# Top-k attention with a ReLU MLP: values as the stationary operand, mask and norm steps on GpSimd, half batches at both ends

## The chip, the cores and the metric

One NeuronCore of a Trainium2 chip runs the whole kernel in one launch. The metric is the time of one execution on the device in microseconds (us). The engines are called by their names in the profile: PE is TensorE (matrix products), DVE is VectorE, ACT is ScalarE, POOL is GpSimd, SP is SyncE, which here only issues DMAs.

## The reference

The attention has 8 batches, 8 heads, 576 tokens and a head size of 64, all float32. Each query keeps the 32 largest of its 576 scores.

```python
scores = scale * np.matmul(q, k.transpose(0, 1, 3, 2))           # 8 x 8 x 576 x 576
kth = np.partition(scores, -32, axis=-1)[..., -32:-31]
scores = np.where(scores >= kth, scores, -1e9)
attn = np.exp(scores - np.max(scores, axis=-1, keepdims=True))
attn = attn / (np.sum(attn, axis=-1, keepdims=True) + 1e-09)
x = heads_side_by_side(np.matmul(attn, v))                       # 8 x 576 x 512
xn = (x - mean(x)) / np.sqrt(var(x) + 1e-06) * g_ln              # over the 512
out = x + np.maximum(xn @ w_ch1, 0.0) @ w_ch2                    # 512 -> 2048 -> 512
```

The two weights come as float64 and are turned to float32 on the chip, word by word.

## The kernel before

**Units.** Two heads of one batch make a pair; there are 32 pairs. A pair has five units: four full query tiles of 128 rows (two score tiles each, one a head) and a rest unit, in which the last 64 rows of both heads share one tile of 128 rows. In all 160 units with 288 score tiles of 128 x 576.

**One unit, in stages.** `scores` (L208, L218): the product of queries and keys of each head, 64 rows deep, as 512 and 64 columns into a score buffer in PSUM, copied to SBUF by ACT. `select` (L229, L238): VectorE finds the 32nd largest score of each row in four rounds of MAX8 with a MATCH_REPLACE8 between them. `weigh` (L246, L249): ACT takes the exponential of all scores, then VectorE keeps those at or above the 32nd in one SCALAR_TENSOR_TENSOR. `values` (L265, L270, L284): TensorE turns the weights (576 columns as four blocks of 128, and the last 64 on their own), ACT copies them out (L273, L274), and each head's five blocks are multiplied with the values; a column of ones beside the values gives the row sum. VectorE inverts the sum (L293, L294) and ACT scales the result into `x` (L297). In this product the turned weights are the stationary operand (128 columns), and values with their ones (65 columns) move.

**The MLP.** When the four pairs of a batch are done, its four tiles of 128 tokens go through `norm` (statistics, centring and scaling at L323, the turn at L329, and gain and PSUM copy in one at L332, all elementwise work on VectorE), 16 `hidden` items (L342, Relu on ACT L350), and one `project` item a tile (16 blocks, L356, residual on VectorE L364). The 64 rest rows of two batches make a fifth tile, done after each odd batch.

**Order.** The source issues, for each unit n, the scores of n + 1, selection and weighting of n, and values of n - 1. MLP items wait in a list `todo` and are popped between the units so that the list is empty at the batch's end; the compiler may move an instruction ahead of one that waits. One piece of weight is decoded a unit in the first 32 units (L110 to L132), on VectorE, GpSimd and ACT; its DMA is issued on GpSimd's queue.

```python
for n in range(N + 1):
    ...
    if 1 <= n < 1 + 2 * NF:
        load_weight(n - 1)
    if n + 1 < N:
        begin(n + 1)
    if n < N:
        select(units[n])
        weigh(units[n])
    if n >= 1:
        finish(n - 1)
```

**Buffers** that matter: two score buffers of two banks (scps), one for turned blocks (tpps), one for the value product (avps) and two for MLP products (mmps) fill PSUM; in SBUF five score tiles, three weight tiles, 17 tiles h for the hidden layer and the weight decoder's scratch.

Of the kernel before, what the change touches and what calls it, by code (L numbers as in the profile page):

```python
# [17 lines left out]
DEN_EPS = 1.0e-9  # L18
LN_EPS = 1.0e-6
J = 4  # L20
# The float64 range that is a float32: the high words of 2^-127 and of 2^128 less
# one, read as float32.
# [5 lines left out]
def kernel(  # L28
# [10 lines left out]
    """Top-k attention per head, then LayerNorm and a ReLU MLP with a residual.  # L39

    Two heads of one batch are taken at a time. Rows 0..511 of a head lie as
    row 4p + j -> partition p, tile j; the last 64 rows are tile 4. Keys and
    values have the same order. The last query rows of both heads share one tile
    of 128 in the selection, and the last rows of two batches share one tile of
    128 tokens (R) in the MLP.
    """
# [8 lines left out]
    DE = D + 1  # L55
# [6 lines left out]

    consts = pool("consts", 1)
    ldpool = pool("ld", 2)
    rawpool = pool("raw", 2)
    kqpool = pool("kq", 2)
    vpool = pool("v", 3)
    scpool = pool("sc", 5)
    wpool = pool("wk", 4)
    epool = pool("e", 3)  # L70
    ptpool = pool("pt", 3)
    small = pool("small", 4)
    xpool = pool("x", 9)
    rpool = pool("r", 2)
    rowpool = pool("row", 3)
# [4 lines left out]
    avps = pool("avps", 1, space=PSUM)  # L80
    mmps = pool("mmps", 2, space=PSUM)
# [12 lines left out]
    def load_weight(i):  # L94
        """A [128, 512] piece of a weight: float64 words to float32, rounded once.

        The high word gives sign, exponent and 20 bits of the mantissa, the low word
        the other 32: w = high part + low * 2^(exponent - 52). Below the float32 range
        it becomes 0, above it the largest float32.
        """  # L100
# [9 lines left out]
        nc.gpsimd.dma_start(raw[:].rearrange("p n w -> p (n w)"), src)  # L110
# [11 lines left out]
        nc.gpsimd.tensor_scalar(size_f, size_f, HIGH_MIN, HIGH_MAX, ALU.max, ALU.min)  # L122
# [9 lines left out]
        nc.gpsimd.tensor_tensor(dst, size_f, low[:], ALU.add)  # L132
# [9 lines left out]

    def load(b, hp):
# [10 lines left out]
        vb = vpool.tile([P, 2, J + 1, DE], FP32, tag="v", name="vb")  # L154
        for hh in range(2):
            rows = v[b, 2 * hp + hh]
            nc.sync.dma_start(
                vb[:, hh, 0:J, 0:D], rows[0:JP, :].rearrange("(p j) d -> p j d", j=J)
            )
            nc.sync.dma_start(vb[0:R, hh, J, 0:D], rows[JP:S, :])  # L160
        nc.gpsimd.memset(vb[:, :, :, D : D + 1], 1.0)
# [3 lines left out]
    def transpose_heads(ins):  # L165
        got = {}
        for name in "kq":
# [8 lines left out]
            nc.scalar.copy(dst[:, 0:JP], ps[:])  # L176
            got[name] = dst
        ps = tpps.tile([P, 512], FP32, tag="tp", name="kqps")
# [6 lines left out]
        for i, name in enumerate("kq"):  # L185
            nc.scalar.copy(got[name][:, JP:S], ps[:, i * R : (i + 1) * R])
        return got["k"], got["q"], ins["v"]

# [1 line left out]

    class Unit:
        def __init__(self, b, hp, qt):
            self.b, self.hp, self.qt = b, hp, qt
            self.rest = qt == J
            self.tiles = [(0, 1)] if self.rest else [(0,), (1,)]

    def scores(u, heads):
        kT, qT, _ = heads
# [3 lines left out]
            scps.tile([P, 1024], FP32, tag="scps", name="scps") for _ in u.tiles  # L202
        ]
        for s0, s1 in ((0, 512), (512, S)):
            for ps, hs in zip(pss, u.tiles):
                for i, hh in enumerate(hs):
                    r = slice(hh * D, (hh + 1) * D)
                    nc.tensor.matmul(  # L208
                        ps[i * R : i * R + ql, s0:s1],
# [11 lines left out]
    def select(u):  # L221
# [3 lines left out]
        for i in range(TOP_K // 8):  # L225
            m = small.tile([P, 2, 8], FP32, tag=f"m{i}", name=f"m{i}")
            tops.append(m)
            for t in range(nt):
                nc.vector.max(m[:, t, :], cur[t][:])  # L229
# [238 lines left out]
```

## Time and profile before

| | |
|---|---|
| three runs | 2334.81, 2338.57, 2341.97 us (median 2338.57) |
| profiled execution, first to last instruction | 2335.4 us |
| TensorE, VectorE busy | 2185.8 us, 1801.5 us |
| ACT, GpSimd busy | 834.5 us, 214.9 us |
| mean granted clock of TensorE | 0.933 |
| MLP products L342 + L356, busy | 581.1 + 521.8 us |
| value product L284, busy | 474.5 us, 3200 instructions |
| scores L208, busy | 407.0 us, 1280 instructions |
| top-k L229 + L238, busy | 826.6 + 704.0 us |
| mask L249, busy | 224.3 us, 288 instructions |

The profile gives one execution. Its own time is known as its span, 2335.4 us, which is 3.2 us below the median of the three runs; what lies around the span isn't listed apart. A group's line reads: source line, engine, operation, output from inputs, their shapes, count, then busy time in all, mean of one in ns, and idle time before them with what ended it. TensorE runs each float32 product as two instructions. Times in the timeline count from the span's start. A window's row lists busy time (and instructions) of PE, weight loads, DVE, ACT and POOL, then the granted clock of TensorE.

### The profile page before, as it was taken

The page shows a single profiled execution, that of the slowest core. Times are in us where ns is not written, and L with a number is a line of the kernel's source. Part 1 is how long each engine was busy: PE and PEld are TensorE (multiplying, and loading weights), DVE is VectorE, ACT ScalarE, POOL GpSimd, SP SyncE. Part 2 cuts the span into 40 slices and gives each one's busy share as a digit, 9 for nine tenths or more (in the row PEclk, how much of TensorE's full clock was granted, in tenths as well). Part 3 has the DMA queues.
Part 4 walks back from the last instruction along what each step waited for, and adds up shares of the span by engine and source line. Part 5 has one row for each costly group of instructions (what it writes and reads, how often), then busy time and mean ns, then how long its engine had stood idle before and what let it go on. Part 6 is the DMA issues. An engine that isn't in the chain of part 4 may idle for free.

```text
span 2335.4 us, 26208 instructions
## 1 busy us (share of the span) xinstructions
PE 2185.8 (94%) x9073; PEld 1272.4 (54%) x9073; DVE 1801.5 (77%) x3841; ACT 834.5 (36%) x1858; POOL 214.9 (9%) x327
## 2 busy tenths in 40 slices
PE   6888779899999998999999998999999998999998
PEld 3555545555554755555455655555555664555445
DVE  7888989788884788888884798889884788988200
ACT  3333333333351434443341444433341443443100
POOL 2344334310000000000000000000000000000000
PEclk9999668789999978999899997999899997999999
DMA  4111111101000000001000000001000000000000
GB/s 101 33 52 56 51 43 58 36 11 30 20 16 19 20 16 16 16 16 29 19 17 10 25 20 16 16 16 29 18 16 12 25 20 16 6 1 10 9 9 14
DMA packets 126731, 56.23 MB, mean 24 GB/s; under 512 B 117892, under 2 KB 117896, under 8 KB 126600
## 3 DMA queue, kind: packets, MB, share of 16 engines
q1 hardware_dynamic: 121992, 37.78, 6.6%
q0 software_dynamic: 4608, 16.78, 2.3%
q8 instruction: 73, 1.20, 0.2%
q14 instruction: 58, 0.48, 0.1%
HBM read 45.09 MB, written 9.44 MB: 23 GB/s over the span
## 4 chain that ended last, share of the span: by engine, by line
PE 82%; DVE 12%; ACT 2%; issue 2%; POOL 1%; DMA 0%; POOLq 0%; DVEq 0%; ACTq 0%
PE hps L342 22%; PE ops L356 22%; PE av L284 17%; PE scps L208 11%; PE tp L270 6%; DVE wk L238 4%; DVE m L229 4%; PE av L265 2%; PE kqps L171 1%; DVE e L249 1%; PE xps L329 1%; POOL size L122 1%; DVE xT L332 1%; ACT e L246 1%; DMA raw<-in_moe_w_ch_dram 0%
## 5 line engine op out<-in xcount | busy, mean ns | idle before, releaser
L229 DVE MAX8 m<-wk 128x8 f32<-128x576 f32 x864 | 615.4, 747 | 0.3
L342 PE MATMUL hps<-xT,w 128*128 128x512 f32 (+1 forms) x1536 | 581.1, 519 | 6.4 <-DVE xT L332 6.4
L356 PE MATMUL ops<-w,h 128*128 128x512 f32 x1152 | 521.8, 599 | 0.5 <-DVE o L364 0.5
L284 PEld LDWEIGHTS av<-vb,pt 128*128 128x128 f32 (+3 forms) x3200 | 427.7, 201 | 139.6 <-issue 35.4
L284 PE MATMUL av<-vb,pt 128*128 128x65 f32 (+3 forms) x3200 | 474.5, 294 | 12.4 <-ACT pt L273 9.7
L208 PE MATMUL scps<-kT,qT 64*128 64x512 f32 (+3 forms) x1280 | 407.0, 523 | 20.2 <-ACT sc L218 20.1
L238 DVE MATCH_REPLACE8 wk<-m,wk 128x576 f32<-128x576 f32 x576 | 424.1, 742 | 0.3 <-issue 0.3
L218 ACT COPY sc<-scps 128x576 f32<-128x576 f32 x288 | 178.6, 644 | 513.9 <-DVE e L249 257.8
L342 PEld LDWEIGHTS hps<-xT,w 128*128 128x128 f32 x1536 | 252.4, 199 | 188.8 <-issue 170.3
L356 PEld LDWEIGHTS ops<-w,h 128*128 128x128 f32 x1152 | 210.2, 190 | 226.3 <-issue 220.7
L208 PEld LDWEIGHTS scps<-kT,qT 64*128 64x128 f32 (+1 forms) x1280 | 163.7, 202 | 153.4 <-issue 118.3
L246 ACT ACTIVATE e<-sc,bias 128x576 f32<-128x576 f32 x288 | 217.9, 776 | 79.7 <-POOL bias L232 47.3
L274 ACT COPY pt<-tp 128x512 f32<-128x512 f32 x288 | 168.2, 584 | 217.5 <-PE tp L270 217.2
L270 PE MATMUL tp<-ident,e 128*128 128x128 f32 x1152 | 204.9, 302 | 34.0 <-DVE e L249 31.5
L249 DVE SCALAR_TENSOR_TENSOR e<-sc,m,e 128x576 f32<-128x576 f32 x288 | 224.3, 807 | 14.2 <-ACT e L246 13.7
L229 DVE MAX8 m<-sc 128x8 f32<-128x576 f32 x288 | 211.2, 748 | 30.0 <-ACT sc L218 28.8
L270 PEld LDWEIGHTS tp<-ident,e 128*128 128x128 f32 x1152 | 150.8, 155 | 143.7 <-issue 73.9
L350 ACT ACTIVATE h<-hps 128x512 f32<-128x512 f32 (+1 forms) x192 | 93.4, 491 | 341.5 <-PE hps L342 341.2
L238 DVE MATCH_REPLACE8 wk<-m,sc 128x576 f32<-128x576 f32 x288 | 212.9, 743 | 0.4
L364 DVE TENSOR_TENSOR o<-ops,x 128x512 f32<-128x512 f32 x32 | 22.0, 689 | 231.9 <-PE ops L356 231.7
L232 POOL TENSOR_SCALAR bias<-m 128x2 f32<-128x2 f32 (+1 forms) x160 | 44.9, 280 | 1488.6 <-DVE m L229 1115.1
L293 DVE TENSOR_SCALAR rinv<-av 128x2 f32<-128x2 f32 (+1 forms) x160 | 25.1, 157 | 172.6 <-PE av L284 140.7
(55 smaller groups left out, 930.3 us busy)
## 6 DMA issues: line engine op xcount, KB each, us to landing
raw<-in_moe_w_ch_dram POOLq DMA_DIRECT2D x32, 512.0 KB, 4.2
kin<-in_k_dram SPq DMA_DIRECT2D x64, 128.0 KB, 2.6
qin<-in_q_dram SPq DMA_DIRECT2D x64, 128.0 KB, 2.6
vb<-in_v_dram SPq DMA_DIRECT2D x64, 128.0 KB, 2.6
out_dram<-o SPq DMA_DIRECT2D x32, 256.0 KB, 2.2
kin<-in_k_dram SPq DMA_DIRECT2D x64, 16.0 KB, 2.4
qin<-in_q_dram SPq DMA_DIRECT2D x64, 16.0 KB, 2.4
vb<-in_v_dram SPq DMA_DIRECT2D x64, 16.0 KB, 2.4
```

What stands on the lines that cost most here:

```text
L208: nc.tensor.matmul(ps[i * R : i * R + ql, s0:s1], qT[r, q0 : q0 + ql], kT[r, s0:s1], start=True, stop=True,)
L218: nc.scalar.copy(sc[:], ps[:, 0:S])
L229: nc.vector.max(m[:, t, :], cur[t][:])
L238: nc.vector.match_replace(wk[:], m[:, t, :], cur[t][:], LOWEST)
L246: nc.scalar.activation(e[:], sc[:], AF.Exp, bias=u.bias[:, t : t + 1], scale=scale)
L249: nc.vector.scalar_tensor_tensor(out=e[:], in0=sc[:], scalar=u.thr[:, t, 7:8], in1=e[:], op0=ALU.is_ge, op1=ALU.mult,)
L270: nc.tensor.transpose(ps[:, c * P : (c + 1) * P], e[:, c * P : (c + 1) * P], ident[:])
L274: nc.scalar.copy(pt[:, 0:J, :].rearrange("p c j -> p (c j)"), ps[:])
L284: nc.tensor.matmul(av[rows, c0 + hh * DE : c0 + (hh + 1) * DE], pts[t][0:kk, c, i * R : i * R + ql], vb[0:kk, hh, c, :], start=(c == 0), s ...
L342: nc.tensor.matmul(ps[:, 0 : n * P], w1[:, c, f * P : (f + 1) * P], xT[0][:, c, 0 : n * P], start=(c == 0), stop=(c == NC - 1),)
L350: nc.scalar.activation(h[:, 0 : n * P], ps[:, 0 : n * P], AF.Relu)
L356: nc.tensor.matmul(ps[:], hT[f][:, i * P : (i + 1) * P], w2[:, f, :], start=(f == 0), stop=(f == NF - 1),)
```

## The change

- **Values.** Units are gathered in groups: the first two full tiles, and the other two with the rest. Values (64 columns of one head) become the stationary operand, and the turned weights of a whole group (256 or 320 queries) move. The two heads fill the two halves of the output's partitions. The result is head size by queries, and is turned back on TensorE (`place`).
- **Row sums** come from ACT's exponential (accum_out). The mask is applied before it, on GpSimd: scores below the 32nd get -1e30 added.
- **Last 64 keys** of both heads are turned in one transpose; for that, the second head's keys are kept with their last 64 first. Scores are made in two pieces of 288 columns.
- **Norm.** Centring on GpSimd; the gain is multiplied into `w1` when it is decoded; PSUM copies on ACT. The residual is an ACT copy and a GpSimd add.
- **MLP.** `project` is cut in four pieces; items are spread over five slots a unit. Batches 0 and 7 are done in two halves by query tiles, each with its own MLP of two tiles and its own loads of keys, queries and values.
- **Order.** Values lag two units instead of one. Two weight pieces are decoded a unit; their DMAs are issued on SP's queue into one buffer instead of two. Several SBUF pools have fewer buffers; PSUM has three mm buffers and no av buffer.

The core of the diff:

```diff
-    rawpool = pool("raw", 2)
+    rawpool = pool("raw", 1)
...
-    scpool = pool("sc", 5)
-    wpool = pool("wk", 4)
-    epool = pool("e", 3)
-    ptpool = pool("pt", 3)
+    scpool = pool("sc", 3)      # now tiles of [P, 2, S]
+    wpool = pool("wk", 2)
+    epool = pool("e", 2)        # now tiles of [P, 2, S]
+    ptpool = pool("pt", 1)      # now [P, 9, 320]: a whole group
...
-    avps = pool("avps", 1, space=PSUM)
-    mmps = pool("mmps", 2, space=PSUM)
+    mmps = pool("mmps", 3, space=PSUM)
...
-        nc.gpsimd.dma_start(raw[:].rearrange("p n w -> p (n w)"), src)
+        nc.sync.dma_start(raw[:].rearrange("p n w -> p (n w)"), src)
...
-        nc.gpsimd.tensor_tensor(dst, size_f, low[:], ALU.add)
+        if i < NF:
+            nc.gpsimd.tensor_tensor(low[:], size_f, low[:], ALU.add)
+            nc.scalar.mul(dst, low[:], gcol[:, c : c + 1])
+        else:
+            nc.gpsimd.tensor_tensor(dst, size_f, low[:], ALU.add)
...
+    def fill():
+        owed[0] += len(todo) / max(1, slots[0])
+        slots[0] -= 1
+        while todo and owed[0] >= 1.0:
+            owed[0] -= 1.0
+            todo.pop(0)()
...
+    def mask(u):
+        nt = len(u.tiles)
+        u.bias = small.tile([P, 2], FP32, tag="bias", name="bias")
+        nc.gpsimd.tensor_scalar_mul(u.bias[:, 0:nt], u.top[:, 0:nt, 0], -scale)
+        u.e = epool.tile([P, 2, S], FP32, tag="e", name="e")
+        for t in range(nt):
+            nc.gpsimd.tensor_scalar(
+                u.e[:, t], u.sc[:, t], u.thr[:, t, 7:8], MASKED, ALU.is_lt, ALU.mult
+            )
+            nc.gpsimd.tensor_tensor(u.e[:, t], u.e[:, t], u.sc[:, t], ALU.add)
+
+    def weigh(u, t):
...
+        nc.scalar.activation(
+            u.e[:, t], u.e[:, t], AF.Exp, bias=u.bias[:, t : t + 1], scale=scale,
+            accum_out=g.den[:, u.col : u.col + 1],
+        )
+
+    def invert(g, cols):
+        nc.gpsimd.tensor_scalar_add(g.den[:, cols], g.den[:, cols], DEN_EPS)
+        nc.vector.reciprocal(g.den[:, cols], g.den[:, cols])
...
+    def values(g):
+        vb = g.job.heads[2]
+        av = mmps.tile([P, 512], FP32, tag="mm", name="av")
+        for c in range(J + 1):
+            for h in range(2):
+                rows = slice(h * R, (h + 1) * R) if c == J else slice(0, P)
+                blk = 2 * J if c == J else h * J + c
+                nc.tensor.matmul(
+                    av[h * D : (h + 1) * D, 0 : g.nq],
+                    vb[rows, blk, :],
+                    g.pt[rows, blk, 0 : g.nq],
+                    start=(c == 0),
+                    stop=(c == J),
+                )
+        g.oT = otpool.tile([P, GQ], FP32, tag="oT", name="oT")
+        nc.scalar.copy(g.oT[:, 0 : g.nq], av[:, 0 : g.nq])
...
+        def centre(i):
+            xns[i] = rowpool.tile([P, DM], FP32, tag="row", name="xn")
+            nc.gpsimd.tensor_scalar(
+                xns[i][:], xs[i][:], mv[0][:, i, 0:1], rstd[0][:, i : i + 1],
+                ALU.add, ALU.mult,
+            )
...
+            if part == Q - 1:
+                o = rowpool.tile([P, DM], FP32, tag="row", name="o")
+                nc.scalar.copy(o[:], out_ps[i][:])
+                nc.gpsimd.tensor_tensor(o[:], o[:], xs[i][:], ALU.add)
...
+    LAG = 2
+    SLOTS = 5
...
+    for n in range(N + LAG + 1):
...
+        for i in range(2 * n, 2 * n + 2):
+            if i < 2 * NF:
+                load_weight(i)
+        back = units[n - LAG] if 0 <= n - LAG < N else None
...
+            if n + 1 < N:
+                scores(units[n + 1])
+            select(u)
+        fill()
+        parts = turn(back) if back is not None else []
+        prev = units[n - 1] if 1 <= n <= N else None
+        if prev is not None:
+            mask(prev)
+        waits = list(range(len(prev.tiles))) if prev is not None else []
+        for i in range(3):
+            if i < len(parts):
+                parts[i]()
+            if i < len(waits):
+                weigh(prev, waits[i])
+            fill()
+        if back is not None and back.qt == back.group.qts[-1]:
+            values(back.group)
+            fill()
+            place(back.group)
+            if n - LAG in mlp_at:
+                give_mlp(n - LAG)
```

## The prediction

> **What bounds the kernel now.** I read the page's parts 1 and 2 first, then the busy time by stretch, then the timeline of one stretch, then groups and waits.
>
> ```profile
> span 2335.4 us, 26208 instructions
> ...
> PE 2185.8 (94%) x9073; PEld 1272.4 (54%) x9073; DVE 1801.5 (77%) x3841; ACT 834.5 (36%) x1858; POOL 214.9 (9%) x327
> ...
> PE 82%; DVE 12%; ACT 2%; issue 2%; POOL 1%; DMA 0%; POOLq 0%; DVEq 0%; ACTq 0%
> ```
>
> TensorE is busy for 94% of the span and has 82% of the chain that ended last, but the average mixes stages:
>
> ```profile
> core 0: us, PE busy (x) PEld busy (x) DVE busy (x) ACT busy (x) POOL busy (x), PEclk, DMA share, GB/s
> 23.60:310.00 286.40, 232.82 (x792) 151.08 (x792) 251.49 (x546) 100.82 (x221) 99.55 (x96) 0.90 0.17 47
> ...
> 380.00:500.00 120.00, 106.86 (x367) 61.21 (x366) 104.93 (x226) 43.63 (x97) 38.63 (x35) 0.76 0.13 36
> 500.00:580.00 80.00, 79.95 (x347) 45.42 (x345) 63.66 (x135) 28.03 (x64) 1.64 (x8) 1.00 0.08 22
> 608.20:840.00 231.80, 231.02 (x1070) 137.57 (x1070) 173.79 (x367) 88.58 (x203) 5.23 (x19) 1.00 0.08 19
> 840.00:892.00 52.00, 42.18 (x148) 24.95 (x147) 43.51 (x97) 16.78 (x35) 0.99 (x5) 0.60 0.05 11
> ```
>
> Up to 310 us (batch 0, no MLP yet, weights being decoded) VectorE is the fuller engine, and from 380 to 500 us TensorE loses time at a granted clock of 0.76. From 500 us on it is full at clock 1.00 (231.02 of 231.80 us) while VectorE is three quarters busy: here a microsecond of TensorE work taken away is a microsecond gained. At each batch's end comes a gap such as 840 to 892: the MLP list is empty, the next normalization is not ready, the clock falls to 0.60. I put these gaps at about 125 us in all (six, of 11 to 27 us).
>
> ```profile
> 1019.20 1.13 PE L208 MATMUL scps<-kT,qT 64*128 64x512 f32 x4
> 1022.47 2.76 PE L284 MATMUL av<-vb,pt 128*128 128x65 f32 x20
> 1025.16 1.12 PE L356 MATMUL ops<-w,h 128*128 128x512 f32 x2
> ...
> 2178.54 1.80 PE L284 MATMUL av<-vb,pt 128*64 128x65 f32 x20 [0.67 <-ACT pt L274]
> ```
>
> Every fp32 product is two instructions. In an unbroken run (58 of L356 in 25.09 us, by the chain in order of time) one of 512 columns takes 0.43 us, so N columns take 0.43 N/512. Four of 512 in 1.13 us (L208) are more than one engine-wide stream could do (1.7): the two heads sit in different 64-row halves of the array and run side by side. The value product streams only 65 columns (0.055 us) but takes 2.7 us for 20: it is paced by the 128-column weight load, 0.11 us each, and by four changes of array shape of about 0.2 us.
>
> **The change, part by part** (us; a *pair* is a job of two heads: four full query tiles and the 64-row rest).
>
> *Values stationary.* Now 4 x 2.7 + 1.75 (rest: 1.80 at 2178) = 12.55 per pair. After: per group 20 instructions, stationary 128x64, moving 256 or 320 columns, 0.214 and 0.267 each. The heads write to the two 64-column halves, c outside, head inside. If the halves run side by side, as the row halves of L208 do: 10 x 0.214 + 10 x 0.267 = 4.8, with shape changes (2 x 0.45) 5.7; if not, 9.6 + 0.9 = 10.5. Turning the output back adds 4.5 transposes at 0.12 (four of L270 span 0.60, starts 0.11 apart) and a change or two: 0.95. So 6.65 or 11.45: it saves 5.9 or 1.1 a pair. No row shows column halves; I take 5.9, by the nearest row, L208's row halves.
>
> The row at 2178.54 is already 64 columns wide, with one row group: 20 steps of load and product in 1.80 us are 0.09 each, less than the 0.155 us that one such load takes (mean of the 512 loads of that shape in the page's groups by shape), so loads are hidden behind products there. The Trainium skill ("TensorE: Matmul & The Clock Gate", Part 3) speaks for and against: column tiles run together (three of 32 columns: 2.38 times), but a weight load overlaps running matmuls only if its row group differs, and both halves here have the same. By the second rule 40 loads a pair at 0.155 us, 6.2, would be exposed and eat the gain; by the row nothing is, and I go by the row.
>
> *Weights' transposes.* 9 instead of 10 a full unit, 6 instead of 5 a rest unit: saves about 0.5 a pair. *Scores* as 288 + 288 instead of 512 + 64: the same columns. Now 1.83 a unit (starts from 608 to 850 us: 25.6 us for 14 full units, about half side by side); after, eight of 288 columns take 0.96 + 0.3 = 1.26 if all run side by side, 2.2 if none; I take 1.65, between, as now: saves 0.9 a pair (-1.9 to +2.9).
>
> Sum: 5.9 + 0.5 + 0.9 = 7.3 a pair. It counts in the 28 pairs after batch 0, where TensorE is full: **204** (70 without side-by-side columns). The extra half jobs of batch 7 cost it 4 more key and query transposes (1.3 each): **+5**. Two-tile MLP halves have twice the instructions of half the columns, no more time (0.214 against a load of 0.11).
>
> *VectorE.* It loses the mask (L249 224 us), L293, L323, L332, L364 (25, 18, 25, 25). What stays for a full unit is four MAX8 rounds:
>
> ```profile
> 1019.68 1.41 DVE L229 MAX8 m<-wk 128x8 f32<-128x576 f32 x2
> ...
> 1022.46 1.41 DVE L229 MAX8 m<-wk 128x8 f32<-128x576 f32 x2
> 1023.78 1.53 DVE L249 SCALAR_TENSOR_TENSOR e<-sc,m,e 128x576 f32<-128x576 f32 x2
> ```
>
> 3 x 2.78 + 1.41 = 9.75 us, 182 us a batch with statistics, against some 215 of TensorE (four pairs of 21, 130 of MLP and its transposes). So this relief is worth nothing while TensorE is full; it is worth something at the start and the batch ends.
>
> *GpSimd.* Its prices:
>
> ```profile
> L122 POOL TENSOR_SCALAR size<-size 128x512 f32<-128x512 f32 x32 | 65.3, 2041 | 147.8 <-DVE rinv L294 127.9 <-DVE size L120 19.4
> L131 POOL TENSOR_TENSOR low<-low,power 128x512 f32<-128x512 f32 x32 | 40.8, 1276 | 65.7 <-DVE power L130 65.7
> L323 DVE TENSOR_SCALAR xn<-x,mv,rs 128x512 f32<-128x512 f32 x32 | 15.9, 535 | 0.0
> ...
> ACT sc L218 <- DVE e L249: 257.8, 69, 11.3
> ```
>
> A mask tile is one two-operation tensor_scalar and one add over 576: 2.27 + 1.43 = 3.7; a full unit 7.65 with its bias, a batch 138, and 15 for centring (2.04) and residual (1.28): 153 of 215, hidden. No row has a comparison: from below 1.43 (no dearer than the add), from above three times L122, 6.8; I take 2.27. MAX8 takes 747 ns both from 120 to 290 us, where GpSimd is 40% busy, and later when it is idle, so sharing costs nothing.
>
> With one input, L122 takes 3.8 times L323's 535 ns of VectorE. The skill's "GPSIMD Engine Reference", 4.1, also advises against the move, but less sharply: GpSimd twice as slow with two inputs, near line rate with one. By the page a mask tile would be some 2.1 us (an estimate from it), by the rows 3.7; the sum is the same, the margin smaller, and I keep the rows.
>
> *The new wait.* ACT's exponential now waits for the mask. Behind it on ACT stand score copies, Relu (L350) and copies of transposes; TensorE waits for these through one tp, three mm and two score buffers. With two units of lag the mask has about a unit, 11.5 us, to finish its 7.65. ACT already waits 257.8 us for score buffers held by VectorE, without emptying TensorE after 500 us. Cost 0; with the cover gone, up to a mask tile, 3.7 us a unit. ACT's new copies, gain fold, rest scaling and the row sums it now makes come to some 110 us more, on an engine 36% busy: hidden.
>
> *Start.* Weights come two a unit: GpSimd 2 x 4.6 + 7.65 = 16.85 a full unit (VectorE 14.9); the raw loads leave its queue for SP, one buffer instead of two. 32 issues of 0.6 us there stand ahead of the 12 loads of a job, due two jobs later: hidden; if not, a job's first scores come up to 7 us late. The decoder's scratch shares the 17 h buffers with the first hidden layer, which by then holds about 11: enough. Batch 0 is over at 24 + 14 x 16.85 + 2 x 13 + 30 + two units of lag 20 = 336 us, with 151 us of TensorE work done (4 pairs of 21, 10 of extra transposes, half an MLP of 55): 185 lost. Before, TensorE is full from 500 us with about 253 done (7 pairs of 28, 55 of hidden layer): 247 lost. Saves **62** (0 to 100).
>
> *Batch ends.* Centring four tiles takes 4 x 2.04 on GpSimd behind a mask, not 6.1 us in all (2180.3 to 2186.4): +2 to +10 each, eight times; I take **+40** (+16 to +80).
>
> *Tail.* Half of batch 7 is off it, but its TensorE work only moves: no gain while TensorE is full. Last unit: mask 3.7, exponential 0.8, transposes 2, values 3.6, place 1, statistics 1.8, centring 4.1, transposes 2: 19 with little else, against 6 idle now: **+14**.
>
> Sum on the profiled span: 2335.4 - 204 + 5 - 62 + 40 + 14 = 2128. The runs' median is 3 above the span: **2130**.
>
> **Rivals.**
> 1. *The column halves don't run side by side.* 204 becomes 70: 2265 (2200 to 2330). For: no row shows them. Against: L208's row halves.
> 2. *GpSimd sets the pace: slower.* Place: L249's mask, now between the last MAX8 and ACT's exponential. With m for a full unit, GpSimd needs 24 + 147 (weights) + 120 (centring, residual) + 110 (tail) + 144 m. It reaches 2335 at m = 13.4, a comparison of 5.2 us, 2.3 times its estimate; at 5.8 us it is 2520. For: the two-operation row is already 3.8 times VectorE's. Against: L122 has just this shape and needs 2.04.
> 3. *More goes well*: scores all side by side (28 x 2 = 56 more), batch ends no longer than now (40): 2035.
>
> **Chances.** Forecast 0.50 (2070 to 2200), column halves in series 0.20, GpSimd 0.13, more 0.17. A measurement of this kernel can't tell under 0.3% (7 us) from no change. Faster 0.82, same 0.04, slower 0.14 (the GpSimd case and the top of the serial one). Range 2020 to 2360, leaving out the best of 3 and most of 2.
>
> **What would show it.** Values: 20 instructions of 256 columns in 2.6 us (side by side) or 4.7. GpSimd busy near 1400 us, tensor_scalar near 2.27 us; ACT's waits for it short. TensorE still full at clock 1.00 in mid batch, gaps at batch ends. If VectorE or GpSimd is fuller than TensorE from 600 to 2000 us, the reasoning is wrong.

## The result, and the profile after

The changed kernel takes 2456.72 us (median of four runs, 2452.11 to 2458.13), the kernel before 2339.85 us in the same comparison: a ratio of 1.050 (95% interval 1.0482 to 1.0518). It is slower by 5%, where the forecast was 2130 us. A time below that has no interval is that of a single run; runs of one kernel here lie within 0.3% of each other.

The page of the changed kernel, its span and part 1:

```profile
span 2456.4 us, 23307 instructions
...
PE 1926.1 (78%) x7601; PEld 1012.0 (41%) x7601; DVE 1531.4 (62%) x3191; ACT 986.5 (40%) x2330; POOL 1284.8 (52%) x1021
```

TensorE has 260 us less work than before (2185.8), VectorE 270 less (1801.5), and yet the span is 121 us longer. No engine is full: TensorE went from 94% of the span to 78%. When work goes away and time comes, look for a wait. Two answers by stretch, first the kernel before, then the changed one, each from the last statistics of batch 0's tiles to the last statistics of batch 7 (columns as in the prediction: TensorE, weight loads, VectorE, ACT, GpSimd, clock):

```profile
313.00:2183.00 1870.00, 1798.57 (x7822) 1043.48 (x7821) 1532.22 (x3263) 712.14 (x1590) 100.55 (x210) 0.93 0.08 20
```

```profile
412.00:2359.00 1947.00, 1611.01 (x6398) 822.90 (x6398) 1236.55 (x2595) 813.99 (x1940) 1010.68 (x791) 0.90 0.07 18
```

TensorE was not busy for 71 us of the first stretch and for 336 us of the second. The three parts of the span add up to the loss: up to batch 0's statistics 313 and now 412 (+99), the middle 1870 and 1947 (+77), the tail after batch 7's statistics 152 and 97 (-55); +121 in all.

The groups of the changed kernel (busy us, mean ns | idle before, releaser), answering to the rows that priced the change:

```profile
L303 POOL TENSOR_SCALAR e<-sc,m 128x576 f32<-128x576 f32 x288 | 642.6, 2231 | 405.6 <-PE tp L363 283.7
...
L313 ACT ACTIVATE e<-e,bias 128x576 f32<-128x576 f32 x288 | 223.2, 775 | 719.5 <-POOL e L306 719.3
...
L306 POOL TENSOR_TENSOR e<-e,sc 128x576 f32<-128x576 f32 x288 | 402.4, 1407 | 16.1
...
L267 PE MATMUL scps<-kT,qT 64*128 64x288 f32 (+3 forms) x1344 | 292.0, 468 | 44.7 <-ACT sc L276 40.1
...
L379 PE MATMUL av<-pt,vb 128*64 128x256 f32 (+3 forms) x1280 | 211.1, 454 | 8.0 <-ACT pt L357 5.3
```

The durations are as estimated: comparison 2.23 us, add 1.41 us. What the estimate had at zero is the last column of L313: before the exponentials, ACT stands still for 719 us, waiting for GpSimd's add. The waits list of the changed kernel gives the same wait, and others (us in total, times, longest):

```profile
ACT e L313 <- POOL e L306: 719.3, 243, 8.1
DVE m L288 <- ACT sc L276: 590.4, 79, 28.9
...
POOL e L303 <- PE tp L363: 283.7, 88, 10.0
...
PE xo L412 <- ACT oT L387: 94.5, 39, 4.8
...
PE tp L335 <- ACT pt L346: 80.2, 40, 5.1
...
DVE den L320 <- POOL den L319: 77.7, 30, 15.0
...
PE tp L354 <- ACT pt L339: 57.8, 19, 5.6
...
PE tp L335 <- ACT e L313: 51.3, 11, 10.4
```

TensorE's own waits (PE) are in the list too: for the output copy oT, for the copies of turned weights pt, which empty the one turning buffer, and, less, for the exponential's result itself.

An idle ACT at 40% would cost nothing by itself. What it costs shows in the timeline of one stretch in the attention of batch 4 (start, duration, engine, line, what it does, [idle before it, and who ended that]):

```profile
1209.69 0.27 PE L363 MATMUL tp<-ident,e 128*128 128x128 f32 x1
...
1210.06 4.56 POOL L303 TENSOR_SCALAR e<-sc,m 128x576 f32<-128x576 f32 x2 [4.96 <-PE tp L363]
...
1213.33 2.53 PE L379 MATMUL av<-pt,vb 128*64 128x256 f32 x20
1214.70 2.76 POOL L306 TENSOR_TENSOR e<-e,sc 128x576 f32<-128x576 f32 x2
...
1216.14 0.77 ACT L313 ACTIVATE e<-e,bias 128x576 f32<-128x576 f32 x1 [5.50 <-POOL e L306]
...
1217.50 0.77 ACT L313 ACTIVATE e<-e,bias 128x576 f32<-128x576 f32 x1 [0.49 <-POOL e L306]
...
1218.27 0.58 ACT L476 ACTIVATE h<-hps 128x512 f32<-128x512 f32 x1
1218.75 0.36 ACT L387 COPY oT<-av 128x256 f32<-128x256 f32 x1
1219.00 0.58 ACT L216 COPY kT<-kqps 64x512 f32<-64x512 f32 x1
...
1219.17 0.44 PE L412 MATMUL xo<-ident,oT 128*128 128x128 f32 x2 [2.73 <-ACT oT L387]
...
1225.92 1.18 ACT L276 COPY sc<-scps 128x576 f32<-128x576 f32 x2 [0.62 <-PE scps L267]
...
1226.59 1.42 DVE L288 MAX8 m<-sc 128x8 f32<-128x576 f32 x2 [25.50 <-ACT sc L276]
```

Read it downwards. The last transpose of an earlier unit (1209.69) frees an e buffer; only now can GpSimd begin the mask, which takes until 1217.5. The two exponentials stand at the head of ACT's queue: ACT is idle for 5.50 us before the first. Behind them, three copies that had nothing to do with this mask run one after the other as soon as the exponentials are through: a hidden tile, the group's output oT, and the next pair's keys. TensorE stood 2.7 us for oT. Five more copies of keys and queries follow, then the scores (1224 to 1226), and VectorE, out of scores since 1201.1, starts again at 1226.59 after 25.5 us.

### The profile page after: what moved, and what is told of

It is laid out like the page before. It is cut to its first block, busy times and chain, and to the rows that moved or that the text cites. A ratio compares the mean times of both kernels' runs of the same rounds, so it can differ in the third digit from the quotient of the medians.

```text
span 2456.4 us, 23307 instructions
## 1 busy us (share of the span) xinstructions
PE 1926.1 (78%) x7601; PEld 1012.0 (41%) x7601; DVE 1531.4 (62%) x3191; ACT 986.5 (40%) x2330; POOL 1284.8 (52%) x1021
## 5 line engine op out<-in xcount | busy, mean ns | idle before, releaser
L303 POOL TENSOR_SCALAR e<-sc,m 128x576 f32<-128x576 f32 x288 | 642.6, 2231 | 405.6 <-PE tp L363 283.7
L468 PE MATMUL hps<-xT,w 128*128 128x512 f32 (+2 forms) x1792 | 598.1, 477 | 9.4 <-ACT h L476 6.2
L483 PE MATMUL ops<-w,h 128*128 128x512 f32 x1152 | 565.7, 626 | 1.4 <-ACT o L492 1.4
L313 ACT ACTIVATE e<-e,bias 128x576 f32<-128x576 f32 x288 | 223.2, 775 | 719.5 <-POOL e L306 719.3
L306 POOL TENSOR_TENSOR e<-e,sc 128x576 f32<-128x576 f32 x288 | 402.4, 1407 | 16.1
L468 PEld LDWEIGHTS hps<-xT,w 128*128 128x128 f32 x1792 | 316.5, 209 | 181.4 <-issue 154.9
L267 PE MATMUL scps<-kT,qT 64*128 64x288 f32 (+3 forms) x1344 | 292.0, 468 | 44.7 <-ACT sc L276 40.1
L335 PE MATMUL tp<-ident,e 128*128 128x128 f32 x1152 | 203.6, 304 | 157.0 <-ACT pt L346 80.2
L379 PE MATMUL av<-pt,vb 128*64 128x256 f32 (+3 forms) x1280 | 211.1, 454 | 8.0 <-ACT pt L357 5.3
L346 ACT COPY pt<-tp 128x512 f32<-128x512 f32 x256 | 150.5, 588 | 113.8 <-PE tp L335 112.8
L476 ACT ACTIVATE h<-hps 128x512 f32<-128x512 f32 (+2 forms) x224 | 97.7, 443 | 142.9 <-PE hps L468 142.0
L379 PEld LDWEIGHTS av<-pt,vb 128*64 128x64 f32 (+1 forms) x1280 | 91.3, 148 | 124.4 <-issue 78.0
```

The lines of the kernel that those rows point to most:

```text
L267: nc.tensor.matmul(ps[i * R : i * R + ql, s, o : o + width], qT[r, q0 : q0 + ql], kT[r, k0 : k0 + width], start=True, stop=True,)
L303: nc.gpsimd.tensor_scalar(u.e[:, t], u.sc[:, t], u.thr[:, t, 7:8], MASKED, ALU.is_lt, ALU.mult)
L306: nc.gpsimd.tensor_tensor(u.e[:, t], u.e[:, t], u.sc[:, t], ALU.add)
L313: nc.scalar.activation(u.e[:, t], u.e[:, t], AF.Exp, bias=u.bias[:, t : t + 1], scale=scale, accum_out=g.den[:, u.col : u.col + 1],)
L335: nc.tensor.transpose(ps[:, c * P : (c + 1) * P], u.e[:, t, k0 : k0 + P], ident[:])
L346: nc.scalar.copy(g.pt[:, t * J : (t + 1) * J, q0 : q0 + P], ps[:].rearrange("p (c n) -> p c n", n=P),)
```

## The experiments

The expectations speak of five theories. **A**: the mask is late on GpSimd, and ACT's exponential waits for it with the copies behind it that TensorE and VectorE need. **B**: the next job's keys and queries are turned only one unit before they are used. **C**: two e buffers hold the mask back. **D**: halved batches, with two weights a unit, make the first batch long. **E**: a step moved to another engine or queue is slow in some other way. A stands beside the mask's place in all that follows; the diffs are against the changed kernel unless another is named.

### Where the mask is computed

```diff
-            nc.gpsimd.tensor_scalar(
+            nc.vector.tensor_scalar(
...
-            nc.gpsimd.tensor_tensor(u.e[:, t], u.e[:, t], u.sc[:, t], ALU.add)
+            nc.vector.tensor_tensor(u.e[:, t], u.e[:, t], u.sc[:, t], ALU.add)
```

> Both mask instructions of every tile go to VectorE, nothing else. Theory A (the mask is late on GpSimd; ACT's exponential stands waiting for it with the copies that TensorE needs behind it): ACT's wait for the mask falls from 719 us to under 200, TensorE's half-clock time from 596 us to under 400, the time to 2200-2320 us, although VectorE's work grows by some 390 us (288 x (0.6 + 0.75)). Theory B (keys and queries of the next job are turned only one unit before use): VectorE's idle time ahead of a job's first unit stays near 480 us and the time at 2430-2500. Theory C (two e buffers hold the mask back): ACT's wait shrinks only with the mask's length, time 2350-2420.

Measured: 2249.06 us, 208 less than the changed kernel, and 89 less than the kernel before beside it (2337.69). The two groups and the wait of this kernel:

```profile
L306 DVE TENSOR_TENSOR e<-e,sc 128x576 f32<-128x576 f32 x288 | 208.2, 754 | 0.2
L303 DVE TENSOR_SCALAR e<-sc,m 128x576 f32<-128x576 f32 x288 | 145.1, 535 | 33.1 <-PE tp L363 33.0
```

```profile
ACT e L313 <- DVE e L306: 323.7, 104, 9.1
```

Theory A's time came true; its wait (under 200 us) and half clock (under 400 us, measured 459) did not fall so far. A tile's mask takes 1.29 us here and 3.64 us on GpSimd. VectorE's busy time rises by 319 us (to 82% of the span), and the time falls: the engine that the change relieved had the room all along.

With the comparison alone moved to VectorE, the add left on GpSimd:

> Only the comparison of the mask (tensor_scalar, 2.23 us on GpSimd) goes to VectorE, where it took 0.54; the add (1.41) stays on GpSimd. A full unit's mask on GpSimd falls from 7.3 to 2.8 us. Theory A (the length of the mask between selection and exponential is what costs, with ACT standing behind it): between the two kernels in proportion to the length left, 2249 + (2457 - 2249) x 2.8/7.3 = 2330, and ACT's wait for the mask some 450 us. Theory E (it isn't the length but the step over to another engine and its queue, with small GpSimd instructions such as the row sums queued behind masks): over 2400.

Measured: 2321.31 us, the exponential's wait 442.9 us. A tile's mask is 0.60 + 1.51 = 2.11 us in this run, and the three kernels lie on one line: 1.29, 2.11 and 3.64 us a tile give 2249, 2321 and 2457 us. One microsecond of mask ahead of the exponential costs 88 us in either step, of the 288 it would cost if every tile's mask lay on the path.

The same step put into the kernel before, without anything else of the change (the two GpSimd instructions ahead of the exponential instead of VectorE's one after it):

```diff
# against the kernel before
-            nc.scalar.activation(e[:], sc[:], AF.Exp, bias=..., scale=scale)
-            nc.vector.scalar_tensor_tensor(out=e[:], in0=sc[:], scalar=u.thr[:, t, 7:8],
-                in1=e[:], op0=ALU.is_ge, op1=ALU.mult)
+            nc.gpsimd.tensor_scalar(e[:], sc[:], u.thr[:, t, 7:8], -1.0e30, ALU.is_lt, ALU.mult)
+            nc.gpsimd.tensor_tensor(e[:], e[:], sc[:], ALU.add)
+            nc.scalar.activation(e[:], e[:], AF.Exp, bias=..., scale=scale)
```

> The kernel before with one part of the change alone: the mask as two GpSimd instructions ahead of the exponential, instead of one VectorE instruction after it (224 us of VectorE's work gone). Theory A: a unit's values follow one unit after its selection, so the 7.3 us and ACT's wait land on the path again: 2400-2600. If the mask does harm only in the new order of work: 2250-2340.

Measured: 2696.27 us against 2334.9 beside it, +361, more than either theory said. VectorE's busy time falls to 1632 us, GpSimd's rises to 1249, and the wait of ACT is there too:

```profile
ACT e L250 <- POOL e L249: 816.0, 220, 15.6
```

So the step that costs is the mask on GpSimd ahead of the exponential, in either kernel; the rest of the change was a gain that it hid. Which of the two hurts, the engine or the place, the next runs tell.

### Which consequence of the late mask does the harm

Three could: GpSimd's load as such, the longer way of one tile from selection to turn, or the copies that stand in ACT's queue behind the waiting exponential. First, the load without the exponential's wait (GpSimd writes a spare tile, so the weights stay unmasked; x has 8 buffers and r 1, for its space):

```diff
             nc.gpsimd.tensor_scalar(
-                u.e[:, t], u.sc[:, t], u.thr[:, t, 7:8], MASKED, ALU.is_lt, ALU.mult
+                spare[:], u.sc[:, t], u.thr[:, t, 7:8], MASKED, ALU.is_lt, ALU.mult
...
-            nc.gpsimd.tensor_tensor(u.e[:, t], u.e[:, t], u.sc[:, t], ALU.add)
+            nc.gpsimd.tensor_tensor(spare[:], spare[:], u.sc[:, t], ALU.add)
...
-            u.e[:, t], u.e[:, t], AF.Exp, bias=u.bias[:, t : t + 1], scale=scale,
+            u.e[:, t], u.sc[:, t], AF.Exp, bias=u.bias[:, t : t + 1], scale=scale,
```

> The changed kernel, in which GpSimd does both mask instructions as before, at their full cost, but into a spare tile that nothing reads; exp reads the scores themselves, so the mask is left out of the result. (For the tile's space, x has 8 and r 1 buffers, as in few_x_buffers.) GpSimd's busy time stays near 1285 us; nobody waits for its add. If the 207 us between this kernel and mask_on_vector are the wait alone, the time is 2249 less what VectorE's two mask instructions cost there (its busy time falls from 83% to 62%): 2150 to 2250. If GpSimd's load itself hurts (shared buffers, its own late bias and residuals), it stays above 2350.

Measured: 2204.04 us, with GpSimd busy for 1285.5 us as before. The load is not it, although GpSimd still holds score tiles for which ACT's copies wait 109.3 us.

Then the wait moved off ACT's queue, with the tile's way from selection to turn shorter only by the exponential (0.96 us with its sum): the comparison makes a keep tile, for which the exponential need not wait, and a GpSimd product stands between exponential and turn. The row sums stay unmasked.

```diff
             nc.gpsimd.tensor_scalar(
-                u.e[:, t], u.sc[:, t], u.thr[:, t, 7:8], MASKED, ALU.is_lt, ALU.mult
+                u.keep[:, t], u.sc[:, t], u.thr[:, t, 7:8], 1.0, ALU.is_ge, ALU.mult
             )
-            nc.gpsimd.tensor_tensor(u.e[:, t], u.e[:, t], u.sc[:, t], ALU.add)
...
         nc.scalar.activation(
-            u.e[:, t], u.e[:, t], AF.Exp, ...
+            u.e[:, t], u.sc[:, t], AF.Exp, ...
         )
+        nc.gpsimd.tensor_tensor(u.e[:, t], u.e[:, t], u.keep[:, t], ALU.mult)
```

> The changed kernel with GpSimd's work placed otherwise: its comparison makes a keep tile from scores and threshold beside the exponential, and its second instruction multiplies the keep tile into exp's result, between exp and the turn. Row sums are left unmasked here. The chain selection, comparison, second instruction, turn is as long as before, but ScalarE's exp waits for no GpSimd instruction. Queue theory: what hurts is that exp stands waiting at the head of ScalarE's in-order queue with the copies of scores, keys, queries and outputs behind it; then the time falls to 2200 to 2320. Chain theory: what hurts is that the tile itself comes late to its turn; then it stays above 2400 (2400 to 2480), and the wait shows on TensorE as tp behind GpSimd's e.

Measured: 2193.38 us, a little under the queue theory's range. Its page, and its waits:

```profile
PE 1852.4 (85%) x7601; PEld 980.2 (45%) x7601; DVE 1536.6 (70%) x3191; ACT 992.6 (45%) x2336; POOL 1280.6 (58%) x1021
```

```profile
DVE m L289 <- ACT sc L277: 406.8, 61, 26.1
POOL e L318 <- ACT e L314: 244.2, 61, 13.8
...
PEld tp L337 <- POOL e L318: 63.6, 21, 10.6
...
PE tp L337 <- POOL e L318: 46.0, 11, 10.3
...
PE tp L337 <- ACT pt L348: 27.1, 13, 3.9
...
PE xo L414 <- ACT oT L389: 9.3, 9, 4.3
```

GpSimd does as much work as in the changed kernel and a tile still needs both its instructions before the turn, but now GpSimd waits for ACT, and ACT's exponential no longer for GpSimd's mask. TensorE waits for the tile to turn as long as before (46.0 us against 51.3 for the exponential in the changed kernel), so the tile's own way is not what changed. The other place of GpSimd's work is worth 258 us against its control, the changed kernel with the same buffers:

> The changed kernel with x 8 and r 1 buffers instead of 9 and 2, and nothing else: the control for e_three, mask_unread and mask_after_exp, which take their space from there. If the space costs nothing: 2445 to 2470. If it costs what e_three lost, 2490 to 2505.

Measured: 2451.71 us, as the changed kernel. It is the queue, then: the mask's length costs because ACT stands and waits for it. The slow engine behind the exponential (2193 us) is better than the fast one ahead of it (2249). (The keep tile also lets the comparison start without an e buffer; the third e buffer, below, takes away that wait and gains nothing.) The control's chain of waits, which covers 84% of the span where that of the changed kernel broke off after a tenth, has GpSimd at 27% of the path on an engine that is busy for 52%:

```profile
PE 33%; POOL 27%; DVE 11%; ACT 8%; issue 5%; POOLq 0%; ACTq 0%
```

Which of the copies behind the exponential it is, one run asked, with Relu moved to VectorE:

```diff
-            nc.scalar.activation(h[:, 0 : n * P], ps[:, 0 : n * P], AF.Relu)
+            nc.vector.tensor_scalar(h[:, 0 : n * P], ps[:, 0 : n * P], 0.0, None, ALU.max)
```

> The changed kernel with one edit: the MLP's Relu (L476) is done by VectorE instead of ScalarE. The mask stays on GpSimd. It separates two forms of theory A. A1, the queue: exp stands at the head of ScalarE's queue waiting for the mask, and what hurts is that Relu, which TensorE's second MLP product needs, stands behind it. Then the time falls well below 2418, to some 2350 or less, although exp waits as before (about 700 us for GpSimd's add). A2, the ring: what hurts is the chain of the tile itself (mask, exp, row sums, turn) and the copies of keys, scores and outputs, which stay on ScalarE. Then the time stays within 40 us of 2457, exp's wait stays near 700 us, and VectorE gains some 150 us of busy time.

Measured: 2506.04 us, 49 more, and these waits:

```profile
ACT e L313 <- POOL e L306: 749.7, 257, 7.8
DVE h L476 <- PE hps L468: 369.5, 104, 29.4
```

So taking Relu out of ACT's queue does not help, and the time lies outside both theories' ranges. This run also shows the same fault a second time: Relu now stands at the head of VectorE's queue waiting for TensorE, 370 us, with the selection behind it. Because of this new wait the run alone can't clear Relu.

The waits shown above say more. From the changed kernel to mask_after_exp, TensorE's wait for output copies falls from 94.5 to 9.3 us and that for the copies of turned weights from 138.0 (L346 80.2, L339 57.8) to 30.1 (L348 27.1, L341 3.0); its time not busy falls by 191 us (530 to 339), about the 193 that these two waits lose. For Relu's tiles it waits 6.2 us in the changed kernel. So the copies of outputs and turned weights are the ones that kept TensorE; this is read from the waits, and no run moves these copies alone.

### Attempts to give the mask more room on GpSimd

A third e buffer (C), and the same with the inversion of the row sums issued after the next selection:

```diff
-    epool = pool("e", 2)
+    epool = pool("e", 3)
...
-    xpool = pool("x", 9)
-    rpool = pool("r", 2)
+    xpool = pool("x", 8)
+    rpool = pool("r", 1)
```

> Three e buffers instead of two, so that a mask doesn't wait for the transposes of two units before (room for it: x 9 to 8, r 2 to 1). Theory C: GpSimd's wait for TensorE's last transpose (284 us) goes, ACT's wait for the mask falls under 350 us, time 2300-2380. Theory A: the mask's own 7.3 us stay between selection and exponential; ACT still waits over 400 us, time 2400-2460. Theory B: 2430-2460.

> e_three, with the inversion of the row sums (an add on GpSimd, a reciprocal on VectorE) issued after the next unit's selection instead of ahead of it. In e_three VectorE's reciprocal waited 275 us for GpSimd's add, with the selection behind it. Queue theory, on VectorE's side: that wait took the place of the one for the e buffer; without it the time falls to 2300 to 2420. If the exp's wait on ScalarE sets the pace by itself, the time stays above 2440 and exp still waits about 700 us.

Measured: 2501.99 and 2534.46 us, both slower, the first above every range given. The waits of the first:

```profile
ACT e L313 <- POOL e L306: 713.6, 236, 11.1
POOL e L303 <- DVE m L288: 416.9, 95, 7.5
...
DVE den L320 <- POOL den L319: 275.2, 37, 16.9
POOL e L303 <- PE tp L363: 55.6, 11, 11.0
```

The wait for the e buffer is gone (283.7 to 55.6 us); the mask waits for the selection instead, and the exponential waits as long as ever. VectorE's reciprocal now stands 275 us behind GpSimd's add. With the inversion issued later that wait was still 271.7 us, so the second run did not take it away and says nothing about it. Theory C is not borne out: the wait it names went, and nothing was gained, though the reciprocal's wait came in its place. Why these two are slower than the changed kernel, and not just no faster, stays open.

A lag of three units, the exponential one unit later (with the buffers of e_three):

```diff
-    LAG = 2
+    LAG = 3
...
+        mid = units[n - 2] if 2 <= n <= N + 1 else None
...
-                weigh(prev, waits[i])
+                weigh(mid, waits[i])
```

> Exponential and turning one unit later (lag 3, three e buffers, x 8, r 1), the mask stays on GpSimd. Theory A, if slack can pay for the mask's length: ACT's wait for the mask falls under 300 us, time 2250-2350. If GpSimd's queue order is the cause (three e buffers alone took 2502 and let VectorE wait 275 us for row sums behind masks): 2420 or more.

Measured: 2472.58 us, the exponential's wait 643.6 us. The later place in the source did not loosen it: the mask again waits for the turn (328.4 us), and the exponential still meets it fresh.

### The other parts of the change

Next job's keys and queries turned from the job's first unit (B), then batches 0 and 7 whole (D):

```diff
# job_early
+            if n == u.job.first and ji + 1 < len(jobs):
+                start_job(ji + 1)
...
-            if n + 1 < N and units[n + 1].job is not u.job:
-                start_job(ji + 1)
```

> Keys and queries of the next job are turned at the start of a job, not in its last unit; nothing else. Theory B: VectorE's idle time ahead of the first units of jobs falls from 479 us to under 150, the time to 2250-2360. Theory A: the idle time moves to other units, ACT's wait for the mask stays over 600 us, time 2400-2460.

```diff
# no_halves
-        if b in (0, B - 1):
+        if False:
```

> Batches 0 and 7 are done whole (32 jobs instead of 40), nothing else. Theory D (halved batches with two weight pieces a unit make the first batch long: it ends at 411 us, before at 316): first batch ends 40-80 us earlier, but the tail grows by about 55 us as half of the last MLP comes back to it: time 2430-2480. Theories A and B: the middle, 2100 us of 2456, is unchanged: 2440-2490.

Measured: 2418.22 us (B is worth 38) and 2527.56 us (the halves are worth 71; the time is above both ranges given). In the run without halves, batch 0's statistics end at 391 us instead of 412 (expected: 40 to 80 earlier), and the tail after batch 7's statistics is 156 us instead of 97: halving costs 21 at the start and saves 59 at the end; the rest lies between.

The two remedies together, mask on VectorE and job early, and the same kernel timed four times:

> Mask on VectorE, and keys and queries of the next job turned at the start of a job. Theory B as a second, smaller cause (38 us with the mask on GpSimd): VectorE's idle time for scores (215 us) falls under 100 us, time 2190-2230. If the first cause hid all of B: 2240-2255.

> The same kernel as mask_on_vector_job_early (both mask instructions on VectorE, next job's keys and queries turned from the job's first unit), timed in rounds for an interval: 2190 to 2200, a ratio to the kernel before of about 0.94.

Measured: 2195.56 us, 54 less than with the mask on VectorE alone (VectorE's wait for scores is 135.9 us, not under 100), and timed again 2196.15 (2194.76 to 2196.6), a ratio to the kernel before of 0.940 (0.9384 to 0.9418). On this version, the loops of the value product exchanged, so that one column half is finished before the other:

```diff
# against mask_on_vector_job_early
-        for c in range(J + 1):
-            for h in range(2):
+        for h in range(2):
+            for c in range(J + 1):
```

> The version with mask on VectorE and next job's start early (2195.56), with the values product's two loops exchanged: all key tiles of one head of the pair first, then all of the other, so that consecutive instructions write the same column half. If the column halves ran side by side because the loop alternated them, the 20 instructions of 256 columns of a pair now take about 4.7 us where they took 2.53, some 2.2 us more in each pair of a unit: 28 pairs a batch by 8 batches gives up to 480 us of TensorE's time at most when every pair has five key tiles, less for the short ones; the 640 groups here have 20 instructions for most. The total goes up by 60 to 400 us. If order does not matter, the product stays at 2.5 us and the time within 10 us of 2195.

Measured: 2279.41 us. In its timeline a group's product is

```profile
1219.46 4.96 PE L379 MATMUL av<-pt,vb 128*64 128x256 f32 x20
```

against 2.53 us at 1213.33 above. The column halves ran side by side when the issue alternated between them, and not when one followed the other. There are 64 such groups (1280 instructions), not the 640 that the expectation names. It adds 160 us to the product (373.2 against 213.3 us) and 84 us to the time: in a kernel where TensorE is busy for 86%, a microsecond of its work was worth half a microsecond.

Last, the version that the results point to: no mask ahead of the exponential, and VectorE's single instruction after it, which also sums the rows.

```diff
# against mask_on_vector_job_early: the two mask instructions are gone, and
         nc.scalar.activation(
-            u.e[:, t], u.e[:, t], AF.Exp, ..., accum_out=...
+            u.e[:, t], u.sc[:, t], AF.Exp, ...
         )
+        nc.vector.scalar_tensor_tensor(
+            out=u.e[:, t], in0=u.sc[:, t], scalar=u.thr[:, t, 7:8], in1=u.e[:, t],
+            op0=ALU.is_ge, op1=ALU.mult, accum_out=g.den[:, u.col : u.col + 1],
+        )
```

> The version with next job's start early, and without the two mask instructions: ScalarE takes exp of the scores straight, and one VectorE instruction (scalar_tensor_tensor) compares the scores with the threshold, multiplies the comparison into exp's result, and sums the rows. VectorE's two mask instructions of 535 and 754 ns become one of about 0.75 to 0.9 us for 576 columns: 0.4 to 0.5 us off each of 288, some 120 to 150 us of VectorE's 1851. Theory A: exp no longer waits for a mask at all (its wait for VectorE's add, 256 us, is gone), and VectorE, at 84% of the span, gets shorter: 2100 to 2190. A rival: the multiply now lies between exp and the turn, so the tile's chain is as long as before and the time stays within 20 us of 2195.

Measured: 2124.42 us (2120.44 to 2125.63), a ratio of 0.909 (0.9078 to 0.9107) to the kernel before (2335.43). The group of the new instruction:

```profile
L311 DVE SCALAR_TENSOR_TENSOR e<-sc,m,e 128x576 f32<-128x576 f32 x288 | 230.3, 825 | 65.6 <-ACT e L308 65.3
```

It takes 0.825 us a tile, and 0.08 to read out the sum, against 1.29 us for the two, and no exponential waits for a mask. It is the fastest kernel of this study, 13.5% below the changed one (2456.72). Against that one three things differ: the mask's place and engine, the row sums, now VectorE's, and the job's early start.

## Why the prediction was wrong, step by step

- **The new wait: the step that failed.** It said "Cost 0; with the cover gone, up to a mask tile, 3.7 us a unit". The right engine, the right queue and the right copies behind it were named, and then priced by the slack of a unit (11.5 us against 7.65). The runs show 243 waits of 3.0 us on average, 719 us in all, and that taking them off ACT's queue is worth 258 us (mask_after_exp against its control). The step compared the mask's time with the lag of its own unit, as if only that unit's turn could suffer; what suffered was what stood behind the exponential in the queue: TensorE waited 94.5 us for output copies and 138.0 for copies of turned weights (9.3 and 30.1 in mask_after_exp), and 51.3 (46.0) for the masked tile itself. And its evidence, 257.8 us of ACT's waiting that emptied no engine, did not carry over: in that same kernel, with the mask on GpSimd, ACT waited 816 us and the time rose by 361 (before_mask_on_gpsimd). In the changed kernel a mask often began late, too, when a turn had freed its e tile (283.7 us of such waits); e_three, nearly without them (55.6), was no faster.
- **The bound of that step was never used.** 3.7 us by 160 units is 592 us, enough to cover what happened; it entered neither the range nor a rival, and the range ended at 2360.
- **Rival 2 had the right place and the wrong mechanism.** It let GpSimd slow the kernel only when its work fills the span, from a comparison of 5.2 us on. The comparison took 2.23 us as estimated, GpSimd was busy for 52%, and the kernel was slower all the same. What decided was the delay of each mask and not GpSimd's throughput; mask_unread, with the same load and no exponential waiting for it, shows it. The sign that the prediction named for a wrong reasoning, VectorE or GpSimd fuller than TensorE from 600 to 2000 us, did not come either: TensorE was busy for 1148 us of these 1400, VectorE for 890, GpSimd for 719.
- **The middle's sum came out near once the wait is gone, by luck.** It was -204 + 5 + 40 = -159. The stretch of mask_after_exp that answers to the two shown above is

```profile
389.00:2093.00 1704.00, 1538.67 (x6384) 790.49 (x6384) 1231.53 (x2588) 816.57 (x1938) 1004.54 (x789) 0.93 0.08 21
```

  that is -166 against 1870. Inside it two terms were off and cancel: TensorE's work falls by 260 us and not 204, and its time not busy rises by 94 (71 to 165) and not 40. In the changed kernel the same stretch is +77.
- **Values: right.** 2.6 us predicted for 20 instructions of 256 columns if side by side, 2.53 measured; 4.7 if in series, 4.96 measured when made so. Rival 1 falls. On the two rules weighed there, the Trainium skill ("TensorE: Matmul & The Clock Gate", Part 3) agrees with the runs on column tiles running together; its rule that a load overlaps only if its row group differs does not describe this product, where 20 loads and 20 products took 2.53 us with 16 of the loads over all 128 rows, one row group. (The prediction's account of the product before, 20 loads at 0.11 us and four changes at about 0.2, makes 3.0 us and not the 2.7 that the row shows.)
- **Scores**: 1.65 us a unit predicted; 1.24 where nothing is waited for (eight of 288 columns at 1237 us, all side by side), 1.91 at 1224, where copies of keys come late. The group fell from 407.0 to 292.0 us, 115 where the sum had 25.
- **GpSimd's prices: right** (2.27 and 1.43 predicted, 2.23 and 1.41 measured), its total 1285 and not 1400: centring took 0.77 us and not 2.04, and the decoder's min and max, whose order the change also swaps, 0.64 instead of 2.04. On "GPSIMD Engine Reference", 4.1, the comparison, with one tensor input, is 4.2 times VectorE's time for the same instruction (2231 to 535 ns), not near it; the add is 1.9 times (1407 to 754), as the page has it.
- **Start: wrong in sign.** It said -62, with batch 0 over at 336 us; its statistics end at 412, 99 later than before (76 later in mask_after_exp). By the prediction's own count of TensorE's work up to there, an estimate, 263 us were lost (412 less 4 x 21 + 10 + 55 = 149). By the same terms the forecast's loss was 187 and the loss before 249; it wrote 185 and 247, which leaves its 62 as it is. GpSimd did not pace it (148 us busy of the 205 from 23 to 228 us). Two things lie in it. All 32 weight pieces are now decoded in this stretch, where before 20 were, at about 3.0 us of VectorE each (2.6 before). And VectorE waits in its own queue for GpSimd's part of the decoding, which stands behind masks (20.4 us before, in its stretch):

```profile
L136 DVE TENSOR_SCALAR size<-size 128x512 uint32<-128x512 uint32 x32 | 14.6, 456 | 74.8 <-POOL size L135 74.8
```

  With the mask on VectorE this wait is 1.7 us and batch 0's statistics end at 370; in threshold_fused they end at 363, so that some 50 of the 99 us have nothing to do with masks on GpSimd.

- **Tail: wrong in sign.** It said +14; the stretch after the last statistics is 55 us shorter, because half of batch 7's MLP no longer stands after the last statistics (no_halves: 156 us instead of 97). The prediction counted that work as only moved into a full TensorE; TensorE was not full. The last unit's own chain, for which the 14 stood, was not measured apart.
- The third rival's time, 2035 us, wasn't reached by any version; the forecast's, 2130, was by threshold_fused, which no longer has the step in question but has a job's early start, and row sums on VectorE, that the change lacks.

## What to carry to other kernels

When an instruction is given a new input from a slow engine, don't ask whether the slow engine keeps up on average; list what stands behind the waiting instruction on its in-order queue. Relief of one engine is lost if it is paid on the queue that empties PSUM for the others: if a slow step must stay, put it after the shared queue's instruction, so that the slow engine waits for the queue and not the queue for it. And price a microsecond of a "full" engine again after the change: in columns_in_series it was worth half of one.

## What the runs showed of the hardware

- GpSimd's time for a one-input tensor_scalar differed with its two operations and their order: for 128 x 512, max then min took 2041 ns (L122 of the kernel before), min then max on the same data 639 ns (L135), add and multiply with a scalar per row 768 ns (L451); comparing and multiplying 128 x 576 took 2231 ns. VectorE needs 535 ns for the last.
- Row sums from ACT's exponential are not free: each comes with an instruction of its own of 0.19 us (ACTIVATION_READ_ACCUMULATOR), 54 us for 288 tiles. On VectorE, in threshold_fused, reading the sum takes 0.08 us, 24 us in all.
- TensorE's granted clock was half for longer where TensorE was idle for longer: 316 us in the kernel before (150 us not busy), 479 in mask_after_exp (339), 596 in the changed one (530). The hidden-layer products (L468, the same mix of shapes) took 477 ns on average in the changed kernel and 457 ns with the mask on VectorE, where the clock was half for 459 us.
